# Weight scales of a recursive matmul layer taken out of the step list that forms its weights, and later fetches cut into pieces

## The chip, the cores and the metric

The kernel runs on one core of a Trainium2 chip. The metric is device time in microseconds for one launch, as the median of several runs. A profile is one execution of the same program, read by the hardware profiler. Five engines work side by side, each from its own queue in order: TensorE (PE: matmuls, with its weight loads in PEld), VectorE (DVE), ScalarE (ACT), GpSimd (POOL) and SyncE (SP), which here only issues transfers. A queue stands still while its first instruction waits.

## The reference, cut to what matters

```python
def _moe_ref(x, w1, w2, w3, w_out):        # x: the attention's output, 1792 x 768
    h = (x @ w1) * (x @ w2) @ w3
    return h @ w_out
def _moe2_ref(x, w_in, w_out):             # w_in 768 x 2048, w_out 2048 x 768
    r = np.maximum(x @ w_in, 0.0)
    return (r * r) @ w_out
```

Talking-heads attention comes first, then these two layers. The change lies in the second one: its input layer is `x @ w_in` with the squared ReLU, its output layer is the product with `w_out`.

## The kernel before, in words

All matmuls of the two layers work on numbers split into a high and a low float16 half; a product of two such numbers takes three matmuls (high by high, high by low, low by high). To split a tensor, it is first scaled by a power of two taken from its largest magnitude; ACT then writes the high half and DVE the low half. The program calls the pair a cast.

**Stages.** Attention fills the first 450 us or so, the hidden layer and a merged weight matrix follow. The product that makes the second layer's tokens (L1179, source `M16` and `hs`) runs next, in four blocks `i` of 448 tokens. The input layer follows (L1782, `multiply_in`), then the output layer (L2004, `multiply`).

**The input layer** uses Winograd's recursive scheme on two by two blocks: seven products in place of eight. It runs 16 items `SEQ[n] = (q, t)`: eight quads `q` (each a pair of 128-column chunks of `w_in`) by two halves `t` of the tokens. An item is seven products of nine matmuls. The last two products of an item (`in3`, `in4`) are issued within the next item. A product's sum is read from PSUM by `take_in` into a tile `ev` (L1817 on ACT, L1819 on DVE) with a scale `scs[n]` (tile `sci`, L1952 on DVE, at the item's start). Product S2 adds onto the tile of A11, and S1 onto that of S2, so TensorE may go on there only when ACT has read the tile.

**What an item needs.** Its quad must be formed: the two chunks are read back from DRAM (`sides`, `ib<-kept_in`, L1016), POOL makes four sums (L1019), and four casts write the quad's halves (L1065 on ACT, L1066 on DVE). Their scale comes from the largest magnitude of a group of four chunks (`top`, L1005): `crossing` sends that number through DRAM, with two transfers that POOL issues (L820, L824), and a DVE chain (`pow2`, L108 to L113) makes the power of two. The tokens need the same: `x2_steps` finds their scale (a PE transpose L1580, a DVE maximum, a PE spread L1588, a DVE chain), then POOL makes sums (L1595) and 21 casts per half write `x` (L1370, L1366). The first half of the tokens lies in `xb`; the mixed output weights are later loaded over it.

**What sets the order.** The program is issued as Python runs, and the order in each queue is written by step lists. A step list (`Stream`) yields pairs of an engine and an estimated cost. `tick(us)` after a product moves an estimated clock `now` and lets every list, in the order of `streams` and the weight decoding last, issue steps whose engine's estimated backlog is at most `ahead[0]` (3 us here). `REST` is a pause in that clock; `after(eng)` is a pause until the engine's estimated backlog is gone. `finish(st)` issues a list's remaining steps at once without pauses; `need(key)` does so with the weight decoding, `need_in(q)` with `form_in`. Transfers of results are kept in `puts` and issued on SP's queue when their estimated time has come, or by `flush`. `allow[0]` is how far the decoding of weight chunks may go; `IN_M` sets it for this part.

**Lists that matter here.** `form_in` forms the quads in order, with each group's `top`, `crossing` and scale ahead of its two quads. Before the first item the program calls `need_in(0)` and `need_in(1)`. At quad 0 `form_in` calls `finish(x_of[0])`, the first half's tokens. `mixed_out(0)` makes the mixed output weights for the output layer's first half (L1696, L1700, L1701) and stores them in `ow_d`; `load_mixed` reads them back in one go during item 14 (L1768). `mixed_tokens` reads the squared results back (`gt<-g`, L1880), makes sums on POOL (L1897) and casts `ao` (L1916 on ACT, L1917 on DVE).

Of the kernel before, what the change touches and what calls it, by code (L numbers as in the profile page):

```python
# [10 lines left out]
F32 = mybir.dt.float32  # L11
# [3 lines left out]
ALU = mybir.AluOpType  # L15
# [3 lines left out]
P = 128  # L19
# [15 lines left out]
def talking_heads_attention_moe_moe2(  # L35
# [678 lines left out]
    NA = NFC - 2  # L714
    IN_M = 14
    chunks += [("in", j) for j in range(12)] + [("out", j) for j in range(NA, OG)]
# [232 lines left out]
    def one_steps(i):  # L949
# [15 lines left out]
        if kind in ("in", "out"):  # L965
            sums = in_sums[:, j : j + 1] if kind == "in" else out_sums[j // OG][:, j % OG : j % OG + 1]
            x, ops = decode(t, n, sums)
            yield from read_raw(i, x, ops)
            yield POOL, 0, lambda: put_later(DVE, "kept", (kept_in if kind == "in" else kept_out)[j], x)
            wsp[kind, j] = True  # L970
            return
        x, ops = decode(t, n)
# [22 lines left out]
    def flat(t):  # L995
        return t.rearrange("p a d -> p (a d)").bitcast(F32)

    def form_in():

        for g in range(NF2 // IG):  # L1000
            box = {}
            a = sm.tile([P, 1], F32, tag="im", name="im")

            def top():
                nc.vector.tensor_reduce(  # L1005
                    a, in_sums[:, g * IG : (g + 1) * IG], axis=AX.X, op=ALU.max
                )

            def scale():
                box["scale"] = pow2(largest_sent(box.pop("sent"), 1), 13, "is")  # L1010

# [8 lines left out]

            while ("in", (g + 1) * IG - 1) not in wsp:
                yield REST, 0.5, lambda: need(("in", (g + 1) * IG - 1))
            yield after(ACT)
            yield DVE, 0.3, top
            yield from crossing(a, 1, box, DVE)
            yield DVE, 0.8, scale
            up, lo = box["scale"]
            for q in range(g * IG // 2, (g + 1) * IG // 2):
                if q == 0:
                    while not x_of:  # L1030
                        yield REST, 0.5, lambda: None
                    finish(x_of[0])
                yield POOL, 0, lambda: sides(q)
# [4 lines left out]
                for o, l, r, op in (  # L1038
                    (ta[:, :OH], a21, a22, ALU.add), (ta[:, OH:], ta[:, :OH], a11, ALU.subtract),
                    (tb[:, :OH], a11, a21, ALU.subtract), (tb[:, OH:], a12, ta[:, OH:], ALU.subtract),  # L1040
                ):
                    yield POOL, 1.1, lambda: mix(o, l, r, op)
                if q:
                    while not fin_pool or (q > 2 and over[0] < q - 1):
# [16 lines left out]
                for x, (h, l) in parts:  # L1061
                    n = x.shape[-1] // OH
                    if x is ta:
                        yield after(POOL)
                    yield ACT, 0.5 * n, lambda: nc.scalar.activation(h, x, AF.Copy, scale=up)  # L1065
                    yield DVE, 0.9 * n, lambda: nc.vector.scalar_tensor_tensor(  # L1066
                        l, x, up, h, op0=ALU.mult, op1=ALU.subtract
# [498 lines left out]
    xbig = []  # L1566

    def xop(t, z, k, c):
        if t == 0:
            return xs_[z][:, k, c]  # L1570
        if k == T4:
# [3 lines left out]
    def x2_steps(t, ts, xm):  # L1575
# [45 lines left out]
        )  # L1621
        yield after(DVE)
        yield POOL, 0, turned
        yield REST, 0.3, None
        yield DVE, 0.25, top
        yield REST, 0.3, None
        yield POOL, 0, spread
# [48 lines left out]
    def mixed_out(g):  # L1676
# [21 lines left out]
        def cast(x, h, l, n):  # L1698
            up = box["up"]
            yield ACT, 0.5 * n, lambda: nc.scalar.activation(h, x, AF.Copy, scale=up)  # L1700
            yield DVE, 0.9 * n, lambda: nc.vector.scalar_tensor_tensor(  # L1701
                l, x, up, h, op0=ALU.mult, op1=ALU.subtract
# [49 lines left out]

    def load_mixed():
        finish(mixed[0])
        flush("ow")
        load_part((B11, B21, T2, T3, T1, B22))
        for q in range(NQ):
            ow[0, q] = [ow_s[q // 2][:, k, q % 2] for k in range(7)]

    ow_s = [  # L1760
# [3 lines left out]

    def load_part(ks):
        for k in ks:
            for z in range(2):
                nc.sync.dma_start(ow_s[z][:, k], ow_d[k][:, 2 * z : 2 * z + 2])  # L1768

# [124 lines left out]
    def mixed_tokens():  # L1894
# [4 lines left out]
        for n in range(2 * NTT):  # L1899
# [9 lines left out]
            a21, a22, a11, a12 = (qs[key] for key in ((1, 0), (1, 1), (0, 0), (0, 1)))  # L1909
            yield REST, lambda: max(0.0, qs["at"] + 6.0 - now[0]), None  # L1910

# [32 lines left out]

    need_in(1)
    streams.append(mixed_out(0))
    for n, (q, t) in enumerate(SEQ):
# [10 lines left out]
        if n:  # L1958
            in3(n - 1)
        y = mm(0)  # L1960
        multiply_in(y, n, A12, B21, True)
# [5 lines left out]
        if n and SEQ[n - 1] == (NP2 - 1, 0):  # L1967
            load_mixed()
        if n and SEQ[n - 1] == (NP2 // 2 - 1, 1):
# [3 lines left out]
        st_[n] = event()  # L1973
        take_in(x, n, None, st_[n])
        tick(0.57, 0.65)
        z = zt_[n] = mm(0)
        multiply_in(z, n, S3, T3, True)
        tick(0.57)
        multiply_in(x, n, S1, T1, False)
        s4 = event()  # L1980
        take_in(x, n, None, s4)
        take_in(z, n, s4, s4)
        g_tile(n, 1, 1, s4, DVE)
        tick(0.57, 0.65, 0.68)
        if n == len(SEQ) - 4:
            streams.append(tokens)
    in3(len(SEQ) - 1)
    in4(len(SEQ) - 1)
    load_part((T4,))
    g_scales[1] = Stream(g_scale(1, gms[1]))  # L1990
# [181 lines left out]
```

## Time and profile before

| what | us |
|---|---|
| median of 3 runs | 1275.64 (1274.67 to 1278.06) |
| the profiled execution, own time | 1276.11 |
| the profiled execution, span | 1274.4 |
| TensorE busy in the span | 1219.5 |

The span goes from the first instruction to the last; the profiled execution's own time is 1.7 us longer. Busy TensorE time includes matmuls at a lowered clock, so both idle time and slow time have to be read. The page's clock row gives the granted clock as a share of full speed; a row of matmuls shows the idle time ahead of it in brackets, with the instruction that ended it.

### The profile page before, as it was taken

What the parts mean: (1) busy time and instruction counts of PE and PEld (TensorE: products, weight loads), DVE (VectorE), ACT (ScalarE), POOL (GpSimd) and SP (SyncE); (2) the same over time, 40 slices, a digit from 0 to 9 for tenths busy, and PEclk for the clock granted to TensorE, in tenths of its full rate; (3) what the DMA queues carried; (4) which work ended last, traced back from release to release, by engine and by line L of the source; (5) the groups of instructions that cost most, each with busy time, mean ns of one, the idle gap of its engine ahead of it and who ended that gap; (6) DMA issues with size and microseconds to landing.
All of it is one profiled execution on the core that took longest, in us unless ns stands there. A gap on an engine that the chain in (4) does not pass through costs nothing.

```text
span 1274.4 us, 26177 instructions
## 1 busy us (share of the span) xinstructions
PE 1219.5 (96%) x9884; PEld 747.7 (59%) x9884; DVE 945.5 (74%) x1721; ACT 804.6 (63%) x1626; POOL 594.1 (47%) x585
## 2 busy tenths in 40 slices
PE   8999999999999999999999999987989996999998
PEld 4666776766666655555579754533445553556565
DVE  6988898798799757765756355857777843899773
ACT  6888888888887536554546465756656653666330
POOL 4898798798787300010014005234124402887350
PEclk9999999999999999999999999988999997999999
DMA  6466456555556726655335171633796875757562
GB/s 195 125 166 168 117 156 166 137 143 143 162 162 167 229 57 153 165 126 157 132 103 168 65 186 65 231 111 100 238 254 152 308 265 145 206 167 226 162 188 87
DMA packets 140354, 205.54 MB, mean 161 GB/s; under 512 B 34148, under 2 KB 115172, under 8 KB 140228
## 3 DMA queue, kind: packets, MB, share of 16 engines
q1 hardware_dynamic: 136020, 200.01, 53.7%
q0 software_dynamic: 1072, 1.45, 0.8%
q10 hardware_dynamic: 3136, 2.40, 0.7%
q8 instruction: 78, 1.28, 0.4%
q14 instruction: 48, 0.39, 0.1%
HBM read 115.12 MB, written 50.17 MB: 130 GB/s over the span
## 4 chain that ended last, share of the span: by engine, by line
PE 75%; DMA 8%; DVE 8%; ACT 5%; issue 2%; SPq 1%; POOL 1%; ACTq 0%; DVEq 0%; POOLq 0%
PE mm L1179 20%; PE mm L2004 13%; PE p L284 10%; PE mm L1782 8%; PE o L380 8%; PE mm L1454 5%; PE s L241 5%; PE a L494 4%; DVE x L1366 2%; DMA g<-ev 2%; DMA Bt<-S 2%; PE p L1179 2%; DMA gt<-g 1%; DMA ib<-kept_in 1%; DVE ATl L402 1%
## 5 line engine op out<-in xcount | busy, mean ns | idle before, releaser
L1782 PE MATMUL mm<-x,wq 128*128 128x448 f16 x882 | 179.3, 365 | 25.5 <-ACT ev L1817 13.4
L1179 PE MATMUL mm<-x,w 128*128 128x448 f16 x1044 | 197.7, 352 | 0.0
L1179 PEld LDWEIGHTS <-w 128*128 128x128 f16 x1152 | 112.2, 98 | 104.3
L2004 PEld LDWEIGHTS <-ao 128*128 128x128 f16 x1176 | 115.3, 98 | 83.9 <-issue 4.4
L284 PE MATMUL p<-Bt,wpre_k 120*120 120x448 f32 x360 | 159.0, 559 | 4.3 <-DMA Bt<-S 3.9
L1782 PEld LDWEIGHTS <-wq 128*128 128x128 f16 x882 | 88.4, 101 | 114.9 <-issue 25.7
L380 PEld LDWEIGHTS <-EH 120*112 120x112 f16 (+1 forms) x1440 | 124.4, 130 | 44.7 <-issue 37.3
L353 POOL TENSOR_SCALAR EH<-E,st 120x448 f16<-120x448 f32 (+1 forms) x152 | 113.0, 752 | 46.8 <-DVE st L336 34.8
L402 DVE TENSOR_TENSOR ATl<-o,ATh 112x480 f16<-112x480 f32 x180 | 116.1, 645 | 23.2 <-ACT ATh L396 22.4
L306 ACT ACTIVATE E<-p,st 120x448 f32<-120x448 f32 x180 | 116.0, 644 | 21.8 <-DVE st L298 13.2
L396 ACT CAST ATh<-o 112x480 f16<-112x480 f32 x180 | 101.1, 561 | 44.4 <-PE o L380 39.7
L380 PE MATMUL o<-wph,EH 120*112 120x120 f16 x720 | 124.0, 219 | 1.3 <-DVE ATl L402 1.3
L380 PE MATMUL o<-wph,EL 120*112 120x120 f16 x720 | 122.0, 216 | 0.0
L380 PE MATMUL o<-wpl,EH 120*112 120x120 f16 x720 | 122.0, 216 | 0.0
L365 POOL TENSOR_TENSOR EL<-F,EH 120x448 f16<-120x448 f32 (+1 forms) x90 | 104.2, 1158 | 33.2 <-issue 20.2
L298 DVE TENSOR_REDUCE st<-p 120x1 f32<-120x448 f32 x180 | 110.2, 613 | 2.2 <-PE p L284 1.9
L1179 PE MATMUL mm<-h,M 128*128 128x448 f16 x576 | 109.8, 353 | 0.7 <-ACT M L1370 0.6
L2004 PE MATMUL mm<-x,ao 128*128 128x384 f16 x588 | 98.2, 329 | 4.2 <-ACT ao L1916 2.9
L2004 PE MATMUL mm<-ow,ao 128*128 128x384 f16 x588 | 96.4, 326 | 1.4 <-DVE st L2020 1.4
L380 PEld LDWEIGHTS <-EL 120*112 120x112 f16 x720 | 93.6, 130 | 0.0
L782 DVE SCALAR_TENSOR_TENSOR xa<-zt,xa 128x768 int32<-128x768 int32 (+1 forms) x70 | 70.1, 1001 | 31.1 <-ACT zt L774 27.5
L367 DVE SCALAR_TENSOR_TENSOR EL<-E,st,EH 120x448 f16<-120x448 f32 (+1 forms) x90 | 83.2, 925 | 10.9 <-POOL EH L353 10.5
(262 smaller groups left out, 2518.8 us busy)
## 6 DMA issues: line engine op xcount, KB each, us to landing
Bt<-S SPq DMA_DIRECT2D x176, 210.0 KB
raw<-in_moe_w_out_dram SPq DMA_DIRECT2D x24, 768.0 KB
g<-ev SPq DMA_DIRECT2D x64, 224.0 KB
gt<-g SPq DMA_DIRECT2D x56, 256.0 KB
raw<-in_moe_w_in_dram SPq DMA_DIRECT2D x16, 768.0 KB
raw<-in_moe_w_dram SPq DMA_DIRECT2D x14, 768.0 KB
raw<-in_moe_w_dram SPq DMA_DIRECT2D x16, 512.0 KB
kept_out<-xa SPq DMA_DIRECT2D x16, 384.0 KB
```

The source lines that it names most:

```text
L284: nc.tensor.matmul(pt[: n * H, :S], wpre_k.rearrange("p t g -> p (t g)")[: n * H, : n * H], Bt.pop(u)[: n * H], start=True, stop=True,)
L298: nc.vector.tensor_reduce(nsum[u][:n, 0, j : j + 1], Pp[u][:n, :S], axis=AX.X, op=ALU.max, negate=True)
L306: nc.scalar.activation(e[:n], Pp.pop(u)[:n, :S].rearrange("p (a b) -> p a b", a=EG), AF.Exp, bias=t[:n, 0, j : j + 1], scale=1.0, accum_ou ...
L353: nc.gpsimd.tensor_scalar(seven(EH[u][:n]), Ex[u][:n], inverse(u), 1.0, op0=ALU.mult, op1=ALU.mult)
L365: nc.gpsimd.tensor_tensor(a, f, b, op=ALU.subtract)
L367: nc.vector.scalar_tensor_tensor(a, e, inverse(u), b, op0=ALU.mult, op1=ALU.subtract)
L380: nc.tensor.matmul(pt[:CP, c * n : (c + 1) * n], a[:n, c * CP : (c + 1) * CP], w[:n, :n], start=(i == 0), stop=(i == 2),)
L396: nc.scalar.copy(ATs[s][0][:, :, :, m * NR : m * NR + nr], src)
L402: nc.vector.tensor_tensor(ATs[s][1][:, :, :, a], src, ATs[s][0][:, :, :, a], op=ALU.subtract)
L1179: nc.tensor.matmul(pt[:, :S], w[a][:, cs], x[z][:, sl], start=(c == 0 and i == 0), stop=(c == len(parts) - 1 and i == 2),)
L1782: nc.tensor.matmul(pt[:, :S], w[:, a, c * P : (c + 1) * P], xop(t, b, kb, c), start=(start and c == 0 and m == 0), stop=(c == 2 and m == 2 ...
L2004: nc.tensor.matmul(pt[:, :OH], y[:, a, q * P : (q + 1) * P], ow[g, q][kb][:, w], start=(start and q == 0 and m == 0), stop=(q == NQ - 1 an ...
```

## The change

The scale of each group gets a step list of its own (`in_scale`), started when the group's last chunk is decoded. `form_in` reads a quad's chunks and makes its sums as soon as those two chunks are decoded, and asks for the scale only ahead of the casts. `need_in(1)` ahead of the items goes, and `finish(x_of[0])` within `form_in` becomes a pause until that list has ended (it is still called when the list is forced). `IN_M` is 16 instead of 14. The token scale's list gets pauses ahead of its two PE steps. Three DVE cast costs are estimated at 0.55 instead of 0.9. The mixed output weights are read back in seven pieces, in the order in which the output layer uses them (`USE`; the first half of the tokens is laid out in the same order), one after each product that read the tokens below them for the last time. The second token tile of the output layer is fetched in item 15, the `mixed_tokens` list starts one item earlier, and its first tile pauses 10 us after its fetch instead of 6.

```diff
-    IN_M = 14
+    IN_M = 16
...
             wsp[kind, j] = True
+            if kind == "in" and j % IG == IG - 1:
+                scaling.append(Stream(in_scale(j // IG)))
+                streams.append(scaling[-1])
...
+    scaling, in_scales = [], {}
+
+    def in_scale(g):
+        box = {}
+        a = sm.tile([P, 1], F32, tag="im", name="im")
...
+        def scale():
+            in_scales[g] = pow2(largest_sent(box.pop("sent"), 1), 13, "is")
+
+        yield after(ACT)
+        yield DVE, 0.3, top
+        yield from crossing(a, 1, box, DVE)
+        yield DVE, 0.8, scale
+
+    def have_scale(g):
+        need(("in", (g + 1) * IG - 1))
+        finish(scaling[g])
...
-            while ("in", (g + 1) * IG - 1) not in wsp:
-                yield REST, 0.5, lambda: need(("in", (g + 1) * IG - 1))
-            yield after(ACT)
-            yield DVE, 0.3, top
-            yield from crossing(a, 1, box, DVE)
-            yield DVE, 0.8, scale
-            up, lo = box["scale"]
             for q in range(g * IG // 2, (g + 1) * IG // 2):
-                if q == 0:
-                    while not x_of:
-                        yield REST, 0.5, lambda: None
-                    finish(x_of[0])
+                while ("in", 2 * q + 1) not in wsp:
+                    yield REST, 0.5, lambda: need(("in", 2 * q + 1))
                 yield POOL, 0, lambda: sides(q)
...
+                while g not in in_scales:
+                    yield REST, 0.5, lambda: have_scale(g)
+                up, lo = in_scales[g]
+                if q == 0:
+                    while not x_of:
+                        yield REST, 0.5, lambda: None
+                    while x_of[0] in streams:
+                        yield REST, 0.5, lambda: finish(x_of[0])
...
-                    yield DVE, 0.9 * n, lambda: nc.vector.scalar_tensor_tensor(
+                    yield DVE, 0.55 * n, lambda: nc.vector.scalar_tensor_tensor(
...
+    USE = (B11, B21, T2, T3, T1, B22, T4)
+
     def xop(t, z, k, c):
         if t == 0:
-            return xs_[z][:, k, c]
+            return xs_[z][:, USE.index(k), c]
...
         yield after(DVE)
+        yield REST, 2.0, None
         yield POOL, 0, turned
         yield REST, 0.3, None
         yield DVE, 0.25, top
-        yield REST, 0.3, None
+        yield after(DVE)
+        yield REST, 0.8, None
         yield POOL, 0, spread
...
-    def load_mixed():
-        finish(mixed[0])
-        flush("ow")
-        load_part((B11, B21, T2, T3, T1, B22))
+    def load_mixed(i):
+        if i == 0:
+            finish(mixed[0])
+            flush("ow")
...
+        for z in range(2):
+            puts.append((now[0] + 1.5, "mixed", ow_s[z][:, i], ow_d[USE[i]][:, 2 * z : 2 * z + 2]))
...
-            yield REST, lambda: max(0.0, qs["at"] + 6.0 - now[0]), None
+            yield REST, lambda: max(0.0, qs["at"] + (6.0 if n else 10.0) - now[0]), None
...
-    need_in(1)
     streams.append(mixed_out(0))
...
             in4(n - 1)
         if n and SEQ[n - 1] == (NP2 - 1, 0):
-            load_mixed()
+            load_mixed(5)
+        if n == len(SEQ) - 1:
+            load_tokens(1)
+        going = SEQ[n] == (NP2 - 1, 0)
+        if going:
+            load_mixed(0)
...
-        if n == len(SEQ) - 4:
+        if n == len(SEQ) - 5:
             streams.append(tokens)
...
-    load_part((T4,))
+    load_mixed(6)
+    flush("mixed")
```

Pieces 1, 2 and 3 follow the later products of item 13 in the same way, and piece 4 follows `in3` in item 14.

## Rows read from the trace of the kernel before

**Rows 1.** The page: its first line and TensorE's busy time.
```profile
span 1274.4 us, 26177 instructions
...
PE 1219.5 (96%) x9884; PEld 747.7 (59%) x9884; DVE 945.5 (74%) x1721; ACT 804.6 (63%) x1626; POOL 594.1 (47%) x585
```

**Rows 2.** Busy time by stretch: length, busy us (xcount) per engine, clock, DMA share, GB/s.
```profile
1071.00:1271.00 200.00, 194.37 (x1181) 115.47 (x1179) 152.22 (x192) 88.23 (x138) 108.16 (x72) 0.99 0.61 176
833.00:892.00 59.00, 44.30 (x202) 20.78 (x200) 39.62 (x70) 33.88 (x63) 26.11 (x24) 0.86 0.31 93
892.00:948.00 56.00, 54.89 (x290) 28.07 (x287) 44.35 (x78) 37.48 (x75) 10.83 (x10) 1.00 0.85 254
948.00:1018.00 70.00, 63.87 (x324) 32.15 (x325) 55.88 (x92) 44.26 (x82) 33.61 (x28) 0.95 0.72 222
1018.00:1117.00 99.00, 83.05 (x439) 44.29 (x439) 57.54 (x89) 48.54 (x89) 34.49 (x25) 0.91 0.71 206
```

**Rows 3.** Timeline, TensorE, 700 to 1120 us: start, length; idle before, its releaser.
```profile
777.37 0.27 PE L1580 MATMUL mm<-ident,xm 128*1 128x128 f32 x1 [1.62 <-DVE xm L1619]
...
841.55 7.28 PE L1782 MATMUL mm<-x,w 128*128 128x448 f16 x27 [5.10 <-ACT ev L1817]
...
868.41 0.93 PE L1782 MATMUL mm<-x,wq 128*128 128x448 f16 x2 [5.56 <-ACT wq L1065]
...
952.90 0.93 PE L1782 MATMUL mm<-x,wq 128*128 128x448 f16 x2 [4.91 <-ACT wq L1065]
...
1057.58 3.39 PE L1782 MATMUL mm<-x,wq 128*128 128x448 f16 x9 [6.83 <-ACT ev L1817]
1065.68 6.14 PE L1782 MATMUL mm<-x,wq 128*128 128x448 f16 x18 [4.71 <-ACT ev L1817]
...
1084.51 0.78 PE L2004 MATMUL mm<-x,ao 128*128 128x384 f16 x2 [2.94 <-ACT ao L1916]
```

**Rows 4.** Windows of 8 us, TensorE alone: length, busy (xcount), granted clock, DMA.
```profile
952.00:960.00 8.00, 6.19 (x21) 0.61 0.14 31
```

**Rows 5.** Timeline, ScalarE, 740 to 880 us.
```profile
834.61 1.42 ACT L1065 ACTIVATE wq<-ib,is 128x768 f16<-128x768 f32 x2
835.94 1.75 ACT L1065 ACTIVATE wq<-it,is 128x768 f16<-128x768 f32 x2
840.86 0.63 ACT L1817 ACTIVATE ev<-mm,sci 128x448 f32<-128x448 f32 x1 [3.18 <-DVE sci L1952]
```

**Rows 6.** Timeline, VectorE, 740 to 880 us.
```profile
784.43 1.56 DVE L1366 SCALAR_TENSOR_TENSOR x<-tm,xs,x 128x448 f16<-128x448 f32 x1
...
840.62 0.15 DVE L1952 TENSOR_TENSOR sci<-kx,is 128x1 f32<-128x1 f32 x1
...
861.53 1.88 DVE L1366 SCALAR_TENSOR_TENSOR x<-st,xs,x 128x448 f16<-128x448 f32 x3 [0.28 <-ACT x L1370]
...
866.66 0.15 DVE L108 TENSOR_SCALAR is<-acr 128x1 f32<-128x1 f32 x1
```

**Rows 7.** Timeline, GpSimd, 720 to 900 us.
```profile
843.32 0.56 POOL L820 DMA_DIRECT2D across<-im  x1 [4.89 <-DVE om L1683]
```

**Rows 8.** Timeline, VectorE, 880 to 960 us.
```profile
927.75 0.15 DVE L1005 TENSOR_REDUCE im<-isum 128x1 f32<-128x4 f32 x1
```

**Rows 9.** Timeline, SyncE's DMA queue, 840 to 1120 us: start, issuing time.
```profile
945.79 1.21 SPq L1016 DMA_DIRECT2D ib<-kept_in  x2
...
1034.69 7.75 SPq L1768 DMA_DIRECT2D x<-ow_d  x12
...
1044.91 4.74 SPq L1880 DMA_DIRECT2D gt<-g  x4
```

**Rows 10.** Timeline, ScalarE, 960 to 1110 us.
```profile
1054.48 1.50 ACT L1916 ACTIVATE ao<-gt,gs 128x512 f16<-128x512 f32 x2 [9.17 <-DMA gt<-g]
```

**Rows 11.** Windows around the fetches at the layer's end, columns as in group 2.
```profile
1018.00:1040.00 22.00, 21.76 (x116) 11.25 (x116) 15.47 (x27) 13.86 (x29) 0.00 (x0) 1.00 0.60 212
1040.00:1056.00 16.00, 10.75 (x57) 5.47 (x56) 2.15 (x5) 4.19 (x9) 2.27 (x2) 0.93 1.06 371
```

More of the change, by code (lines that the diff above doesn't have):

```diff
@@ L996, in flat, with top @@
         return t.rearrange("p a d -> p (a d)").bitcast(F32)
+    scaling, in_scales = [], {}
+    def in_scale(g):
+        box = {}
+        a = sm.tile([P, 1], F32, tag="im", name="im")
+        def top():
+            nc.vector.tensor_reduce(
+                a, in_sums[:, g * IG : (g + 1) * IG], axis=AX.X, op=ALU.max
+            )
+        def scale():
[7 more added lines that the diff above has]
+        finish(scaling[g])
     def form_in():
@@ L1001, in form_in @@
             box = {}
[L1002 to L1010, printed above, removed]
             def sides(q):
@@ L1700, in cast @@
             yield ACT, 0.5 * n, lambda: nc.scalar.activation(h, x, AF.Copy, scale=up)
-            yield DVE, 0.9 * n, lambda: nc.vector.scalar_tensor_tensor(
+            yield DVE, 0.55 * n, lambda: nc.vector.scalar_tensor_tensor(
                 l, x, up, h, op0=ALU.mult, op1=ALU.subtract
@@ L1751, in mixed_out @@
         return mixed[g]
-    def load_mixed():
-        finish(mixed[0])
-        flush("ow")
-        load_part((B11, B21, T2, T3, T1, B22))
-        for q in range(NQ):
-            ow[0, q] = [ow_s[q // 2][:, k, q % 2] for k in range(7)]
     ow_s = [
@@ L1763, in talking_heads_attention_moe_moe2 @@
     ]
[L1765 to L1768, printed above, removed]
+    def load_mixed(i):
+        if i == 0:
+            finish(mixed[0])
+            flush("ow")
+            for q in range(NQ):
+                ow[0, q] = [ow_s[q // 2][:, USE.index(k), q % 2] for k in range(7)]
+        for z in range(2):
+            puts.append((now[0] + 1.5, "mixed", ow_s[z][:, i], ow_d[USE[i]][:, 2 * z : 2 * z + 2]))
     gms = [sm.tile([P, OG, B], F32, tag="gm", name="gm") for _ in range(2)]
@@ L1959, in talking_heads_attention_moe_moe2 @@
             in3(n - 1)
+            if SEQ[n - 1] == (NP2 - 1, 0):
+                load_mixed(4)
         y = mm(0)
@@ L1974, in talking_heads_attention_moe_moe2 @@
         take_in(x, n, None, st_[n])
+        if going:
+            load_mixed(1)
         tick(0.57, 0.65)
@@ L1977, in talking_heads_attention_moe_moe2 @@
         multiply_in(z, n, S3, T3, True)
+        if going:
+            load_mixed(2)
         tick(0.57)
         multiply_in(x, n, S1, T1, False)
+        if going:
+            load_mixed(3)
         s4 = event()
```

## The prediction

> **What bounds the kernel now.** First the page: TensorE is busy 96% of the span [rows 1], so only its idle and its slow time can be won. Then the windows by stage, where the reader is to see that the loss is local. In the undisturbed stretch, 892 to 948, 290 matmuls of 448 columns take 54.89 us of busy time at full clock, 0.189 us each; the output layer's 384 columns take 194.37 / 1181 = 0.165 us [rows 2]. Against these rates:
>
> - 833 to 892 (the input layer's first items): idle 59.0 - 44.3 = 14.7 us; 202 matmuls should take 38.2 us and take 44.3, so 6.1 us are slow clock (0.86).
> - 892 to 948: idle 1.1 us, clock 1.00.
> - 948 to 1018: idle 6.1 us; 324 matmuls should take 61.3 and take 63.9, 2.5 us slow.
> - 1018 to 1117 (the seam of the two layers): idle 15.9 us; some 200 matmuls of 448 columns and 239 of 384 should take 77.2 us and take 83.05, 5.9 us slow.
>
> That is 52.4 us, and 1.6 us stand ahead of it at 777. Next the timeline of TensorE, for what ended each gap [rows 3]: an eviction by ACT (5.10 at 841, 6.83 and 4.71 at 1057 and 1065), a quad's cast (5.56 at 868, 4.91 at 952), a token cast (2.94 at 1084). Last the 8 us windows: the one that follows the gap at 952 ran at 0.61, close to the lower level of 1.2 GHz [rows 4], while the 1.1 us lost before 948 left the clock at 1.00 [rows 2]. So a long gap costs twice and a short one once.
>
> **The change part by part.**
>
> *Token scale pauses.* The transpose at 777 waited 1.62 us on DVE [rows 3]. With 2.0 us of pause it is issued later, among matmuls that have work. Bounds: 0 to 1.6 gained. What hides it is the running product; if the DVE chain is later than the pause, a part comes back. I take 1.2.
>
> *need_in(1) gone (gap at 841).* ACT ran quad 1's four high halves at 834.6 to 837.7, then waited 3.18 us for `sci`, which stood on DVE behind the four low halves [rows 5, 6]; only then came the eviction that TensorE waited for. After the change `sci` is issued ahead of those casts. But the casts aren't gone: `form_in` may issue them at the first two ticks, and their estimated ACT cost of 3.5 us fits nearly whole into the 3 us of backlog allowed. So ACT still runs about 3.1 us of casts first, and the eviction ends near 834.6 + 3.1 + 0.6 = 838.4 instead of 841.5. The gap shrinks from 5.1 to about 2.0. Bounds: 0 left if the casts land behind the eviction, 5.1 if nothing changes.
>
> *Scales apart (gaps at 868 and 952).* Group 1's number left for DRAM at 843.3 [rows 7] and its scale chain started at 866.7 [rows 6]: 23 us, all of it after quad 1's casts, and quad 2 waited for it. Group 2's `top` ran at 927.8 [rows 8], quad 4's chunks were asked for only at 945.8 [rows 9], and TensorE stood at 948. Now the number of group 1 can travel from the moment its fourth chunk is decoded; `IN_M` 16 lets that happen in block 1 instead of block 2. The crossing leaves the path, and reads and sums of a quad follow the last quad's casts directly: for quad 4 some 18 us earlier (945.8 - 927.8). What is late next is the quad itself: fetch, POOL sums, casts, and for quads 3 on the wait for a free tile.
>
> *The first items get crowded.* This is what I charge against the gain. DVE is busy 39.6 us in 833 to 892 [rows 2], and TensorE needs only 38.2 us there at full rate. One chunk's decoding (about 2.5 us of DVE) moves ahead of 833 with `IN_M`, so 37 us of DVE must fit into 38. The second half of the tokens has to be ready at item 3, and its list stands ahead of the quads in the order. I leave 5 us of waits beside the 2.0, and 3 us of slow clock. Bounds: 0 and the 12.7 idle now left over (14.7 - 2.0); I take 5 since the work just fits. The stretch then gives 20.8 - 10 = 10.8 us.
>
> Here the Trainium skill speaks against the change. A token cast on DVE takes 1.56 us while POOL makes sums (784.4) and 1.88 / 3 = 0.63 us when it doesn't (861.5) [rows 6]. The Trainium skill, SBUF — State Buffer, section "Who interferes with whom", says that GpSimd and VectorE share one port pair and that it is an exclusive lock; the rows agree in direction. By that rule the 26 us of POOL in this stretch can't lie under DVE's two-operand work, and a shorter stretch packs them closer: at worst the stretch stays near 50 us and gives 9 instead of 10.8, a sum 1.8 us higher.
>
> *948 to 1018.* With quad 4's reads 18 us earlier the 4.91 should go but for a remainder; quads 5 to 7 gain likewise. I leave 1.8 us idle and 0.7 slow of 8.6: gain 6.1. Bounds: 0 (the fetch is as late as before, behind other entries of SP's queue) and 8.6. The stretch 892 to 948 I leave as it is.
>
> *DVE estimates of 0.55.* They remove no instruction and add none; the lists may issue more DVE work per tick, and an eviction or `sci` can stand behind more of it. Cost: nothing where TensorE has 27 matmuls (5.1 us) between a product and the next use of its tile, all of it in a rival below.
>
> *Fetches in pieces, earlier.* SP issued the twelve reads of the output weights in one block from 1034.7 to 1042.4 and the first tokens' four reads right behind it, from 1044.9 [rows 9]. Their `ao` cast stood at the head of ACT's queue for 9.17 us, until 1054.5 [rows 10], with evictions behind it: hence 6.83 and 4.71. In that time the DMA engines were full (share 1.06 in 1040 to 1056) while 1018 to 1040 had 40% free [rows 11]. The pieces start an item earlier, the last weight chunks are decoded two items earlier, and the first tokens' fetch no longer follows a block of twelve. Each piece waits on SP's queue for the product that reads its tile; behind it wait result stores and the tokens' fetch, a few us at most. The twelve reads carry 4.7 MB, at 371 GB/s 12.7 us of the engines; the free share before 1040 is 8.8 us, so some 4 us still fall where they did. I leave 4 us idle at the seam, 1.5 at 1084 and after (the second tile is fetched an item earlier), 2.5 slow, 8 of 21.8: gain 13.8. Bounds: 0 and 21.8.
>
> Sum: 1.2 + 10.8 + 0 + 6.1 + 13.8 = 31.9. The profiled execution took 1276.1 us, 0.5 above the median of the runs: 1276.1 - 31.9 = 1244.2, so 1244 for the median.
>
> **The rivals.**
>
> 1. *The gaps move.* The crossing goes, but quads 2 and 4 are then late by fetch and sums, the first items are DVE-bound, and `ao` still waits for a full DMA. For it: DVE 39.6 against 38.2, DMA share 1.06. Against it: from 892 to 948 the same kinds of casts, fetches and evictions ran with 1.1 us idle. The stretches give 5, 2 and 5 us with the 1.2: 1276 - 13 = 1263. Chance 0.20.
>
> 2. *All cover holds.* Every gap over 2 us goes and the clock stays up: the losses left are about 2 at 836, 1.1, and 5 elsewhere, so 54 - 8 = 46 won: 1230. For it: the clock's share (14.5 us) goes by itself with the long gaps. Chance 0.10.
>
> 3. *Slower: evictions behind a deeper DVE queue.* Place: the starts of items 4 to 12, where `sci` and the last eviction of the item before must pass DVE within 5.1 us. With estimates of 0.55, a backlog of 3 estimated us holds five casts of 384 columns; beside POOL at the 1.56 us of rows 6 that is 7.8 us, 2.7 too many. If every one of 16 items pays it, that is 43 us, all 32 gained and 11 more: 1287. It decides against the change from 2.0 us per item. Against it: DVE was busy 44.3 of 56 us from 892 to 948 [rows 2], so its queue runs empty between, and POOL only 10.8. Chance 0.09.
>
> 4. *The change does nothing measurable:* the lists wait for the same decoding and the forced `need_in` calls restore the old order. 1275. Against it: `sci` and the crossing change place for certain. Chance 0.05.
>
> The forecast itself, 1236 to 1254, has 0.56.
>
> **How the numbers follow.** A difference under 0.3% (3.8 us) can't be told from none. Forecast and rivals 1 and 2 are faster: 0.86; rival 4 is the same, 0.05; rival 3 slower, 0.09. The low end, 1229, takes in rival 2's figure; the high end, 1267, takes rival 1 with all bounds of the seam but the worst. Outside are rivals 3 and 4 and a little of 2, under 0.2.
>
> **What would show it.** In the profile after: no `wq` cast that waits for a scale chain, and `top` of group 1 well ahead of the first item; TensorE's first gap in the input layer near 2 us, ended by ACT; the 833 to 892 work done in about 48 us; output weight reads spread over some 20 us, and an `ao` wait on ACT under 5 us; the clock near 1.0 from the first item to the output layer. Wrong would be: a new wait on `x` casts at item 3 over 8 us; a piece's wait on SP that holds the token fetch; `sci` starting late in the items where nothing waited before.

## The result, and the profile after

The changed kernel took 1258.42 us (median of 4 runs, 1256.89 to 1261.17), the kernel before 1276.2 in the runs beside it (4 runs): 17.8 us less, a ratio of 0.9862 with a 95% interval of 0.984 to 0.9885. The forecast was 1244, the range 1229 to 1267. The sign and the range held; the forecast's own range of 1236 to 1254 didn't, and 14 of the 32 us stayed away. The time lies nearer to rival 1's 1263 than to the forecast, though not for the reason that rival 1 gave.

The profiled execution after took 1261.17, the slowest of its four; its span is 1259.5 us, 14.9 us shorter than the one before, and TensorE is busy 1214.7 us of it.

The stretches of [rows 2] in the kernel after (length; busy us and count of PE, PEld, DVE, ACT, POOL; granted clock, DMA share, GB/s):

```profile
833.00:892.00 59.00, 47.53 (x218) 22.86 (x216) 49.84 (x80) 37.21 (x71) 28.35 (x23) 0.88 0.46 135
892.00:948.00 56.00, 49.74 (x255) 25.07 (x254) 46.93 (x75) 36.89 (x71) 20.48 (x16) 0.97 0.80 261
948.00:1018.00 70.00, 63.61 (x334) 32.54 (x333) 50.83 (x84) 46.63 (x90) 26.91 (x23) 1.00 0.68 218
1018.00:1117.00 99.00, 97.00 (x562) 54.87 (x561) 65.46 (x96) 54.78 (x96) 44.03 (x32) 1.00 0.65 203
```

The stretches hold other work now, so count matmuls: 218 instead of 202 in the first, 255 instead of 290 in the second, 334 instead of 324 in the third. The stretch that I had left as it is lost 35. Only in the fourth did both idle and slow clock go: 97.00 of 99 us busy at 1.00, against 83.05 at 0.91. The timeline of TensorE shows it gap by gap (start, length; idle before, its releaser), the counterpart of [rows 3]:

```profile
841.15 1.28 PE L1800 MATMUL mm<-x,w 128*128 128x448 f16 x3 [5.50 <-ACT ev L1835]
...
870.23 6.95 PE L1800 MATMUL mm<-x,wq 128*128 128x448 f16 x27 [3.17 <-DVE ev L1837]
879.79 2.50 PE L1800 MATMUL mm<-x,wq 128*128 128x448 f16 x9 [2.61 <-ACT ev L1835]
...
920.22 3.56 PE L1800 MATMUL mm<-x,wq 128*128 128x448 f16 x18 [2.76 <-ACT ev L1835]
...
935.95 25.43 PE L1800 MATMUL mm<-x,wq 128*128 128x448 f16 x126 [3.22 <-ACT ev L1835]
964.57 3.56 PE L1800 MATMUL mm<-x,wq 128*128 128x448 f16 x18 [3.19 <-ACT ev L1835]
```

What the reader is to see: no gap is ended by a `wq` cast any more (5.56 and 4.91 before), and from 1018 to 1117 none is over 1.3 us (6.83, 4.71 and 2.94 before). But the gap at 841 stands, and from 870 to 965, where two gaps near 5 us stood before, five of about 3 us wait for an eviction. (Item 4 starts at 895, item 8 at 951, item 13 at 1018.)

To compare kernels whose stages shift, I divide each one's timeline of TensorE by the count of matmuls: item 0 has 45 of 448 columns, every other item 63, and 18 close the layer; the output layer is divided after 588 of its 1176. Each boundary is the start of the first matmul of the next stage. (Interpolating inside a merged row of the timeline isn't good enough: in the kernel before, the row that holds item 13's start also holds the slow clock after the gap at 952, and the boundary comes out 2.4 us late. The expectations below were worked out with boundaries of that kind, so where they have 53.4 us for items 13 to 15 before, the table has 55.8.) The token product is the stage ahead of the input layer. Times are us.

| kernel | token product | items 0-3 | 4-12 | 13-15, tail | output, 1st half | 2nd half | median us | ratio to before (95%) |
|---|---|---|---|---|---|---|---|---|
| before | 112.6 | 66.0 | 116.9 | 55.8 | 101.8 | 97.4 | 1276.2 | |
| after | 110.3 | 63.1 | 122.5 | 40.0 | 100.8 | 97.5 | 1258.42 | 0.9862 (0.984-0.9885) |
| seam_only | 112.6 | 65.7 | 116.4 | 40.1 | 98.3 | 98.8 | 1259.45 | 0.9867 (0.984-0.9894) |
| scales_only | 110.8 | 60.3 | 123.1 | 40.0 | 109.4 | 97.9 | 1266.73 | 0.9927 (0.9905-0.9949) |
| est09 | 112.0 | 64.3 | 110.5 | 40.8 | 95.6 | 100.9 | 1249.02 | 0.9779 (0.9749-0.9809) |
| inm14 | 110.3 | 59.1 | 121.8 | 40.0 | 100.8 | 97.5 | 1254.57 | 0.9831 (0.9803-0.9859) |
| est09_mixed | 111.3 | 61.5 | 116.0 | 40.0 | 95.6 | 99.2 | 1249.74 | 0.9815 (0.9795-0.9835) |
| abs_later | 110.3 | 62.9 | 125.6 | 40.0 | 100.8 | 97.5 | 1264.49 | 0.9926 (0.9914-0.9939) |
| no_pause | 112.0 | 59.6 | 124.0 | 40.0 | 100.8 | 97.8 | 1259.69 | 0.9881 (0.9864-0.9897) |
| est09_inm14 | 110.3 | 60.0 | 117.5 | 41.8 | 99.9 | 99.2 | 1250.56 | 0.9826 (0.9805-0.9848) |
| ahead_lo | 114.4 | 66.0 | 116.5 | 40.0 | 102.0 | 98.9 | 1262.9 | 0.9915 (0.9897-0.9933) |
| est09_gact | 114.5 | 58.6 | 114.9 | 44.9 | 95.5 | 98.9 | 1253.34 | 0.9837 (0.9817-0.9856) |
| est09m_inm14 | 110.3 | 59.1 | 113.9 | 41.2 | 95.6 | 100.7 | 1246.81 | 0.9787 (0.9767-0.9807) |
| est09m_gact | 111.8 | 59.2 | 115.7 | 40.0 | 95.6 | 100.8 | 1248.66 | 0.9801 (0.978-0.9821) |

One of est09's six runs, 1271.35 us at a granted clock of 0.945, was slow and is left out of its median and ratio.

At 0.189 us a matmul the three stages of the input layer would take 44.3, 107.3 and 39.1 us without a loss. So the layer's end is now clean (40.0), items 0 to 3 are 19 us over and items 4 to 12 are 15 over. Between the two profiled executions the stages give 2.3 + 2.9 - 5.5 + 15.8 + 1.0 - 0.1 = 16.4; the unchanged stretch ahead of the token product was 1.5 longer after, which leaves the 14.9 of the span.

How well does one execution's stage repeat? The kernels after, scales_only and est09_mixed give every engine and SyncE's queue the same instructions in the same order from the token product to the end of item 3. There they took 110.3, 110.8 and 111.3 us in the product and 63.1, 60.3 and 61.5 us in items 0 to 3, and the first gap of the input layer, 5.50 us in the kernel after, was shorter in the two others (scales_only first):

```profile
836.68 0.73 PE L1801 MATMUL mm<-x,w 128*128 128x448 f16 x3 [2.75 <-ACT ev L1836]
837.58 0.73 PE L1800 MATMUL mm<-x,w 128*128 128x448 f16 x3 [3.42 <-ACT ev L1835]
```

est09 and est09_gact share their order through the product, and it took 112.0 and 114.5 us. So a difference of less than some 3 us between two stages of single executions shows nothing by itself.

### The profile page after: what moved, and what is told of

It reads as the page before. It is cut to its first block, busy times and chain, and to the rows that moved or that the text cites. A ratio compares the mean times of both kernels' runs of the same rounds, so it can differ in the third digit from the quotient of the medians.

```text
span 1259.5 us, 26176 instructions
## 1 busy us (share of the span) xinstructions
PE 1214.7 (96%) x9884; PEld 747.0 (59%) x9884; DVE 944.1 (75%) x1721; ACT 803.7 (64%) x1626; POOL 592.3 (47%) x585
## 3 DMA queue, kind: packets, MB, share of 16 engines
q8 instruction: 78, 1.28, 0.4%
## 4 chain that ended last, share of the span: by engine, by line
PE 73%; DVE 13%; ACT 5%; DMA 5%; issue 3%; POOL 1%; SPq 0%; ACTq 0%; DVEq 0%
PE mm L1196 20%; PE mm L2035 10%; PE p L284 9%; PE mm L1800 9%; PE o L380 8%; PE mm L1471 5%; PE s L241 5%; PE a L494 4%; DVE x L1383 2%; DMA Bt<-S 2%; PE p L1196 2%; DVE xa L778 1%; DVE ow L1722 1%; DMA ow_d<-st 1%; ACT wq L1082 1%
## 5 line engine op out<-in xcount | busy, mean ns | idle before, releaser
L1800 PE MATMUL mm<-x,wq 128*128 128x448 f16 x882 | 173.7, 358 | 19.3 <-ACT ev L1835 16.2
L396 ACT CAST ATh<-o 112x480 f16<-112x480 f32 x180 | 101.1, 562 | 46.0 <-PE o L380 40.8
L782 DVE SCALAR_TENSOR_TENSOR xa<-zt,xa 128x768 int32<-128x768 int32 (+1 forms) x70 | 72.7, 1038 | 26.0 <-ACT zt L774 22.3
```

Of the source, the lines that this page charges most:

```text
L396: nc.scalar.copy(ATs[s][0][:, :, :, m * NR : m * NR + nr], src)
L1800: nc.tensor.matmul(pt[:, :S], w[:, a, c * P : (c + 1) * P], xop(t, b, kb, c), start=(start and c == 0 and m == 0), stop=(c == 2 and m == 2 ...
```

## The experiments

My theory after the result: the seam is worth what was forecast, the scales apart are worth little by themselves, and the estimates of 0.55 and `IN_M` 16 cost time that they were charged nothing for. The rival: one of the two large parts works against the other, and neither number matters.

**seam_only.** The kernel before with the fetches in pieces alone:

```
+    USE = (B11, B21, T2, T3, T1, B22, T4)
+        if n == len(SEQ) - 1: load_tokens(1)
+        going = SEQ[n] == (NP2 - 1, 0)
+        if going: load_mixed(0)      # pieces 1 to 6 likewise
-        if n == len(SEQ) - 4:
+        if n == len(SEQ) - 5:
             streams.append(tokens)
```

> The kernel before with the later fetches alone: mixed output weights read back in seven pieces, token tile 1 fetched in item 15, the token list one item earlier with its 10 us. If the seam's gain stands by itself (theory): the last three items drop from 53.4 to about 40 us, and the output layer isn't slowed by denser casts, so about 1276 - 13 - 4 = 1259. If it needs the earlier decoding that IN_M 16 brings (rival): the first token tile is still late, 1268 to 1272.

Measured: 1259.45, with items 13 to 15 at 40.1 instead of 55.8. The seam alone gives as much as the whole change (ratios 0.9867 and 0.9862). Which of its three edits does it (pieces, the token list an item earlier, the second tile in item 15) was not taken apart.

**scales_only.** The kernel after without these fetches: pauses, `in_scale`, `IN_M` 16, 0.55, no `need_in(1)`.

> The changed kernel without the later fetches: scale lists apart, no need_in(1), IN_M 16, pauses, estimates of 0.55. Theory (the scale part gives back by new waits in items 4 to 12 and in the output layer what it wins at 777 and in items 0 to 3): 2.3 + 2.9 won, 3.1 and about 3 lost, so 1274 to 1278, no change. Rival (the two parts help each other, the seam hides nothing of this part): 1266 to 1270.

Measured: 1266.73, so my theory fell. The time is the rival's, but its reason, that the parts help each other, isn't seen. The scale part isn't worth nothing: it empties items 13 to 15 too (40.0), and it pays 7.6 us in the first half of the output layer (109.4 against 101.8) and 6.2 in items 4 to 12. By ratio the two parts alone win 0.0133 + 0.0073, some 26 us; together 17.8. They overlap by about 9 us, and the place is the seam: over items 13 to 15 and the output layer's first half seam_only wins 19.2 us, scales_only 8.2 and both together 16.8.

**est09.** The kernel after with the old estimates:

```
-                    yield DVE, 0.55 * n, lambda: nc.vector.scalar_tensor_tensor(
+                    yield DVE, 0.9 * n, lambda: nc.vector.scalar_tensor_tensor(
```

in `form_in` and in `mixed_out`'s cast. The change lowers the estimate in these two lines, not in three. Nothing else differs: the same instructions, issued at other points.

> The changed kernel with the three VectorE estimates back at 0.9. Theory (the lists issue casts too densely at 0.55; ScalarE's sum in the weight decoding and evictions then wait behind them): the new waits of 2.8, 3.2 and 3.2 us in items 5 to 10 shrink to under 1 each and the output layer's 1.3 us waits per token tile go, so 1246 to 1251. Rival (the waits come from the work packed together, GpSimd sums beside VectorE casts, whatever the estimate): 1256 to 1260, the waits stay.

Measured: 1249.02; its interval lies below that of the change. Items 4 to 12 take 110.5 instead of 122.5 us, and the first half of the output layer 95.6 instead of 100.8. Waits of TensorE from 700 to 1260 us by releaser (us in total, times, longest), the kernel after first:

```profile
PE mm L1800 <- ACT ev L1835: 21.7, 11, 5.5
PE mm L2035 <- DVE st L2051: 5.3, 5, 1.3
```

and est09:

```profile
PE mm L1800 <- ACT ev L1835: 8.9, 7, 3.2
PE mm L1800 <- DVE x L1383: 5.8, 1, 5.8
PE mm L1800 <- ACT x L1387: 3.3, 1, 3.3
PE mm L2035 <- DVE st L2051: 3.2, 2, 2.5
```

Waits for evictions fall from 21.7 to 8.9 us (of those expected to shrink to under 1, 1.20 and 1.67 us are left at 920 and 984). What appears instead is a wait for the second tokens' casts at item 3 (5.8 and 3.3).

**inm14.** The kernel after with `IN_M = 14`.

> The changed kernel with IN_M back at 14. Theory (the two chunks decoded ahead of the input layer hold ScalarE back, so the eviction of item 0 starts 2.7 us later than the casts alone make it): the first gap falls from 5.5 to about 2.5 us, but the same decoding then lies in items 1 to 4; 1255 to 1258. Rival (the earlier decoding is what makes the seam's fetches early): the first tokens come later and the seam loses 3 to 8 us, 1261 to 1266.

Measured: 1254.57, and items 0 to 3 at 59.1 instead of 63.1; the gap at 841 becomes 1.52 (at 835.8). The totals' intervals overlap, so only the stage tells it. It is 59.1 in est09m_inm14 too, which has the same order there, and the first gap is 1.52 in all three runs with 14. Against the three executions of one order named above (60.3 to 63.1) the gain is 1.2 to 4.0 us.

**est09_mixed.** Only `mixed_out`'s cast gets its 0.9 back.

> The changed kernel with the estimate of 0.9 in mixed_out alone; form_in keeps 0.55. Theory (it is the mixed output weights' casts that fill VectorE's queue in items 4 to 12 and in the output layer, since 28 of them are issued per layer half): nearly all of the gain of the run with all estimates at 0.9, items 4 to 12 near 111 us instead of 122 and the first half of the output layer near 96 instead of 101; 1248 to 1251. Rival (the quads' casts ahead of the items are the ones that block): 1254 to 1258.

Measured: 1249.74. The first half of the output layer comes down to 95.6 by this alone, items 4 to 12 only to 116.0. By ratio 6 of est09's 10.6 us come from this one number; the other 4.6 aren't certain, since the two intervals overlap. Over all runs the number decides items 4 to 12: the six with 0.9 here take 110.5 to 117.5 us, the five with 0.55 and the old limit on the backlog 121.8 to 125.6.

**abs_later.** A theory of how 0.55 costs: in items 4 to 12 ScalarE takes a step of a chunk's decoding (`zt`) that waits for VectorE, with an eviction behind it on ScalarE. The step is put 2.5 us later:

```
         x, ops = decode(t, n, sums)
+            ops.insert(-1, (REST, 2.5, None))
```

> The changed kernel with one more pause of 2.5 us in the decoding of the second layer's weight chunks, ahead of ScalarE's sum of magnitudes; estimates stay at 0.55. Theory (that sum stands at the head of ScalarE's queue while VectorE is late, and the evictions wait behind it): ScalarE's waits for the decoded chunk fall from 7.8 to under 2 us in 890 to 1020, and items 4 to 12 from 122 to 114 to 117 us; the output layer keeps its 1.3 us waits; 1250 to 1254. Rival (VectorE is late in any case and the evictions wait for its scale product or for the tiles it frees): items 4 to 12 stay at 120 or more, 1256 to 1260.

Measured: 1264.49, slower; the theory fell. ScalarE's waits from 890 to 1020 us in the kernel after:

```profile
ACT zt L789 <- DVE xa L782: 7.8, 4, 2.8
ACT ev L1835 <- DVE sci L1969: 7.3, 4, 4.4
```

and in abs_later, where lines are one higher:

```profile
ACT ev L1836 <- DVE sci L1970: 12.4, 6, 4.6
```

The wait of `zt` is gone, and ScalarE now waits more for `sci` and, in its ReLU, for VectorE's own eviction (7.0 us against 4.3). So ScalarE's order was a symptom: it waits for a VectorE that is late, whichever operation stands at the head.

**no_pause.** The token scale pauses taken out again (`REST, 2.0`, `after(DVE)`, and 0.3 for 0.8).

> The changed kernel without the two pauses in the token scale's list. Theory (the pauses alone took the 1.6 and 0.5 us ahead of the two steps on TensorE at 777, and 1.1 at 851): the token product goes from 110.3 back to 112.5 us and items 0 to 3 lose about 1; 1260 to 1262. Rival (the list is no longer forced, so the steps come apart without the pauses): 1257 to 1259.

Measured: 1259.69, not to be told from the change. The product is back at 112.0; the small products of the two token scale chains wait 1.65 us at 782 and 4.2 at 840, and items 0 to 3 still take only 59.6.

**est09_inm14.** Both numbers back.

> The changed kernel with all VectorE estimates at 0.9 and IN_M at 14. Theory (the two are independent: 9.2 from the one, 3.9 from the other): 1244 to 1247. Rival (with 0.9 the first items are no longer held by the two chunks ahead of them, so 14 only makes the later decoding late): 1248 to 1252.

Measured: 1250.56, as the rival had it. The two gains don't add: items 0 to 3 come to 60.0, and items 4 to 12 are 117.5 instead of 110.5. The loss lies in items 4 to 7 (56.9 against 49.0). That the chunks decoded later cause it isn't shown: est09_gact, with `IN_M` 16, has 55.0 there.

**ahead_lo.** The rival on 0.55: not which list is dense, but how much work may stand in VectorE's queue. The limit scaled down with the estimates (3.0 times 0.55 / 0.9 is 1.83; I took 1.65):

```
-    ahead[0] = 3.0
+    ahead[0] = 1.65
```

> The changed kernel with estimates of 0.55 but a backlog of 1.65 us allowed instead of 3.0 from the token product on, so that as many casts may stand in VectorE's queue as with 0.9 and 3.0. Theory (the depth of VectorE's queue ahead of an eviction is what costs): items 4 to 12 fall from 122 to about 112 us and the output layer's 1.3 us waits per token tile shrink; 1247 to 1253. Rival (what costs is that the list of the mixed output weights runs off too early and too fast, whatever the depth): items 4 to 12 stay above 119, 1255 to 1262.

Measured: 1262.9, slower than the change. Items 4 to 12 improve to 116.5, between what the two sides expected, but the product (114.4), items 0 to 3 (66.0) and the output layer pay for it. The limit holds for every list, 0.55 only for two, so this run doesn't tell whether depth ahead of an eviction is what costs in items 4 to 12.

**est09_gact, est09m_gact.** Items 0 to 3 keep VectorE busy, so eight of their ReLU tiles go to ScalarE, on top of est09 and est09_mixed:

```
-        g_tile(n, 0, 0, s1, DVE)
+        g_tile(n, 0, 0, s1, ACT if n < 4 else DVE)
-        g_tile(n, 1, 1, s4, DVE)
+        g_tile(n, 1, 1, s4, ACT if n < 4 else DVE)
```

> The run with all estimates at 0.9, and in items 0 to 3 the two squared-ReLU tiles that VectorE made per item are made by ScalarE: 8 tiles of about 0.7 us leave VectorE. Theory (items 0 to 3 are bound by VectorE, busy 48 of 59 us there): they fall from 64 to 58 to 60 us, 1243 to 1246. Rival (ScalarE's own evictions, which TensorE waits for first, are what binds): they stay or grow, 1249 to 1255.

> Estimate 0.9 in mixed_out alone, and the squared-ReLU tiles of items 0 to 3 on ScalarE. Theory (VectorE binds the first items): items 0 to 3 fall from 61.5 to 57 to 59 us, 1245 to 1248. Rival (ScalarE's evictions bind): 1250 to 1255.

Measured: 1253.34 and 1248.66. Items 0 to 3 come down as expected (58.6 and 59.2), but with est09 the total is no better: items 4 to 12 (114.9) and the layer's end (44.9) take more than in est09. The 114.5 of the product isn't the edit's, for the product's order is est09's. With est09_mixed the total can't be told from est09_mixed itself.

**est09m_inm14.** 0.9 for `mixed_out` alone, and `IN_M` 14.

> Estimate 0.9 in mixed_out alone, 0.55 in form_in, IN_M at 14. Theory (with the quads' casts issued early, the two chunks fewer shorten items 0 to 3 as they did with 0.55 everywhere): 1245 to 1248. Rival (as with 0.9 everywhere, the decoding that is put off lands in items 4 to 7): 1249 to 1253.

Measured: 1246.81, the lowest median: 2.1% under before, and its interval lies wholly below that of the change. Against est09 it is not shown to be faster (0.9787 and 0.9779). Its largest gaps left in the input layer are two waits for token casts at item 3 (3.22 us at 873.7 and 2.60 at 876.8) and one for an eviction at 914.6 (3.10).

## Why the prediction was right in sign and short in size

**The sum.** By stage: token product 1.2 us forecast, 2.3 measured; items 0 to 3, 10.8 and 2.9; items 4 to 12, 6.1 forecast and 5.5 lost; the seam, 13.8 and 16.8. Two terms fell 8 and 12 us short. That the total stayed in its range owes 3 us to a seam that gave more than its term.

**The seam: right, and a little more.** 13.8 us forecast up to 1117; 15.8 measured in items 13 to 15 and 1.0 in the first half of the output layer. SyncE's queue after (start, issuing time) shows the twelve reads of [rows 9] in four steps over 15 us, and the first tokens' fetch ahead of them instead of behind:

```profile
1000.10 2.17 SPq L1898 DMA_DIRECT2D gt<-g  x4
1021.80 0.80 SPq L1161 DMA_DIRECT2D x<-ow_d  x2
1025.20 5.18 SPq L1161 DMA_DIRECT2D x<-ow_d  x6
1033.15 0.98 SPq L1161 DMA_DIRECT2D x<-ow_d  x2
1036.55 0.80 SPq L1161 DMA_DIRECT2D x<-ow_d  x2
```

The first `ao` casts ran from 1015.8 with no wait, where 9.17 us stood in [rows 10]. I left 8 us of loss there; 2 are left (99.0 - 97.0). That the part is worth this by itself, seam_only shows (15.7 and 3.5).

**The token pauses: right in sign.** 1.2 forecast; 1.3 to 2.3 in the three executions of the same order, of which no_pause gives back 0.7 to 1.7. That is near what one execution differs by, so the size isn't shown. In est09, with the pauses, the product took 112.0.

**need_in(1): the move happened, its gain didn't.** I had ScalarE run 3.1 us of casts from 834.6 and the eviction right behind, a gap of 2.0. `sci` did come early, and the scale chain with it (VectorE):

```profile
829.70 0.15 DVE L108 TENSOR_SCALAR is<-acr 128x1 f32<-128x1 f32 x1
...
834.10 0.15 DVE L1969 TENSOR_TENSOR sci<-kx,is 128x1 f32<-128x1 f32 x1
```

The casts took their 3.1 us, but started at 837.50, for ScalarE was late (its timeline):

```profile
826.52 0.91 ACT L774 ACTIVATE zt<-raw 128x768 f32<-128x768 f32 x1 [2.80 <-DMA raw<-in_moe_w_in_dram]
...
831.32 0.84 ACT L789 ACTIVATE zt<-xa 128x768 f32<-128x768 f32 x1 [2.67 <-DVE xa L782]
...
837.50 1.43 ACT L1082 ACTIVATE wq<-ib,is 128x768 f16<-128x768 f32 x2
838.83 1.75 ACT L1082 ACTIVATE wq<-it,is 128x768 f16<-128x768 f32 x2
840.49 0.61 ACT L1835 ACTIVATE ev<-mm,sci 128x448 f32<-128x448 f32 x1
```

The two chunks that `IN_M` 16 lets in just ahead of the layer cost 5.47 us of waits at ScalarE's head, one of them for a chunk's transfer. In scales_only, with the same order, these two waits are 1.33 and 2.15 us and the gap is 2.75: part of the 5.50 is this execution's bad luck. I had counted one chunk's decoding moved out of the first items as relief; inm14 shows that it moved onto their first eviction: without it the gap is 1.52.

**Scales apart, 833 to 892: the crossing left the path, the size failed.** Group 1's maximum is taken at 808.8 and its scale stands at 829.7, both ahead of item 0, and the 5.56 us wait on `wq` is gone. I left 10 us of loss (2.0 for the first gap, 5 for crowding, 3 for slow clock) and kept a gain of 10.8; items 0 to 3 won 2.9, in scales_only 5.7. The first gap (5.50 instead of 2.0, but 2.75 in scales_only) is 0.8 to 3.5 of what is missing. VectorE is a likely bound for a part: it was busy 49.84 us of the 59, against 39.62 before, for only 16 more matmuls. But with ReLU tiles moved off it (est09_gact) it was busy 36.0 of 58.6 us and the stage was still 14 us over the ideal, so its load alone doesn't explain what remains; that wasn't settled.

**"DVE estimates of 0.55 ... cost nothing": the step that failed.** It is the place that rival 3 named, evictions behind a deeper VectorE queue in items 4 to 12, at a smaller price: est09 shows 12.0 us there and 5.2 in the first half of the output layer, 3.4 of them given back in the second, where rival 3 had 43. I set it at nothing because a product has 5.1 us of cover at each tile, and because VectorE was busy only 44 of 56 us. The average hid where the work lands. The 28 casts of `mixed_out`'s first half ran on VectorE from 914.1 to 1000.1 before, from 910.1 to 971.6 after, and from 910.6 to 999.7 in est09, and the last store left SyncE's queue at 1007.17, 972.32 and 998.79: with 0.55 the list starts no sooner but ends some 30 us sooner, and is denser. The gap at 935.95 in the kernel after, VectorE first:

```profile
926.23 0.94 DVE L1969 TENSOR_TENSOR sci<-kx,is 128x1 f32<-128x1 f32 x1
927.09 1.43 DVE L1722 SCALAR_TENSOR_TENSOR st<-ob,os,st 128x384 f16<-128x384 f32 x1
928.45 1.35 DVE L775 TENSOR_SCALAR xa<-raw 128x768 int32<-128x768 int32 x1
929.72 1.35 DVE L1722 SCALAR_TENSOR_TENSOR st<-ob,os,st 128x384 f16<-128x384 f32 x1
...
932.78 1.63 DVE L782 SCALAR_TENSOR_TENSOR xa<-zt,xa 128x768 int32<-128x768 int32 x1
934.34 0.60 DVE L1722 SCALAR_TENSOR_TENSOR st<-ot,os,st 128x384 f16<-128x384 f32 x1
```

GpSimd at that time:

```profile
925.77 1.37 POOL L1717 TENSOR_TENSOR ot<-ob 128x384 f32<-128x384 f32 x1
927.11 0.99 POOL L1717 TENSOR_TENSOR ot<-ob,ot 128x384 f32<-128x384 f32 x1
928.07 1.31 POOL L1037 TENSOR_TENSOR it<-ib 128x384 f32<-128x384 f32 x1
929.46 1.19 POOL L1037 TENSOR_TENSOR it<-it,ib 128x384 f32<-128x384 f32 x1
...
931.90 1.70 POOL L1037 TENSOR_TENSOR it<-ib,it 128x384 f32<-128x384 f32 x1
```

and ScalarE:

```profile
934.45 0.84 ACT L789 ACTIVATE zt<-xa 128x768 f32<-128x768 f32 x1 [2.49 <-DVE xa L782]
...
935.29 0.61 ACT L1835 ACTIVATE ev<-mm,sci 128x448 f32<-128x448 f32 x1
```

A cast that the list reckons at 0.55 takes 1.35 to 1.43 while GpSimd sums and 0.60 at 934.34, after the last sum ended (931.90 + 1.70). The decoding step on VectorE is late behind them, ScalarE waits 2.49 us for it, and the eviction that TensorE needs comes 3.22 us late. The Trainium skill, SBUF — State Buffer, section "Who interferes with whom", which the prediction weighed at 1.8 us in the first items, states that these two engines share a port pair under an exclusive lock; the rows of this gap agree.

But the longer casts aren't what 0.55 adds. VectorE's casts of this list from 895 to 1018, the kernel after first, then est09 (count; busy us, mean ns of one):

```profile
L1722 DVE SCALAR_TENSOR_TENSOR st<-ob,os,st 128x384 f16<-128x384 f32 x12 | 11.3, 960 | 2.2 <-ACT st L1721 2.2
L1722 DVE SCALAR_TENSOR_TENSOR st<-ot,os,st 128x384 f16<-128x384 f32 x16 | 9.2, 611 | 0.1
L1722 DVE SCALAR_TENSOR_TENSOR st<-ob,os,st 128x384 f16<-128x384 f32 x12 | 11.0, 933 | 2.4 <-ACT st L1721 2.4
L1722 DVE SCALAR_TENSOR_TENSOR st<-ot,os,st 128x384 f16<-128x384 f32 x16 | 9.1, 613 | 4.6 <-ACT st L1721 4.6
```

The same 28 casts cost VectorE the same with either estimate; 0.9 only spaces them. That the spacing is worth the time, est09 and est09_mixed show. Why a denser list delays evictions is read from this one gap, and is not shown for the others.

In the output layer the same list's second half is dense too. VectorE before the gap of 1.28 us at 1115.72:

```profile
1108.48 2.76 DVE L1722 SCALAR_TENSOR_TENSOR ow<-ob,os,ow 128x384 f16<-128x384 f32 x2
1111.17 3.97 DVE L1722 SCALAR_TENSOR_TENSOR ow<-ot,os,ow 128x768 f16<-128x768 f32 x2
1115.06 0.60 DVE L2051 SCALAR_TENSOR_TENSOR st<-mm,sv,st 128x384 f32<-128x384 f32 x1
```

Four casts in a row, 6.7 us, stand ahead of an eviction; three such gaps of 1.28 us follow each other at 15.5 us.

**948 to 1018: the wait went, the gain only in est09.** 6.1 us forecast here and nothing in 892 to 948; items 4 to 12 lost 5.5. The wait of 4.91 on `wq` is gone, as forecast. With the old estimates they won 6.4 in est09, the forecast's size, but the five other runs with 0.9 in `mixed_out` lie between 0.6 lost and 3.0 won. So the term was covered by the one above, and how much of it is there without 0.55 isn't settled.

**Rivals.** Rival 1 came nearest in time; its first half (items bound by VectorE) is seen at most in part, its second (`ao` still waits for a full DMA) isn't seen at the seam. Rival 2's clean profile didn't come. Rival 4 is out by the interval.

**Open.** Why est09 and inm14 don't add is shown only as to place (items 4 to 7), not as to cause, and no run here tells what keeps items 0 to 3 at 58.6 us and more.

## What to carry to other kernels

In a hand-written order the cost estimate of a filler operation is a spacing: lowering it to the operation's duration alone made the same work end sooner and in clumps here, so change it in a run of its own, and look at which stage the clump lands in. Charge a step that is moved ahead of a stage to the queue that runs into that stage, not only as relief to the one it leaves. Two edits that each clear the same stall aren't worth their sum; run each alone before adding terms. Before a stage's few microseconds are explained, look for two kernels with the same order there and see how far they differ.

## What the runs showed of the hardware that was not expected

The lengthening beside GpSimd's sums doesn't go by size. The 128x1 product `sci`, with two tensors as operands, took 0.94 us at 926.23, inside the sum that began at 925.77, and 0.15 at 834.10. Of the 16 in the kernel after, five took 0.94 to 1.07 us, each begun inside a sum, and the others 0.16 at most (two of 16 in the kernel before). VectorE's timeline at 851.75:

```profile
851.75 1.07 DVE L1969 TENSOR_TENSOR sci<-kx,is 128x1 f32<-128x1 f32 x1
...
852.93 0.15 DVE L109 TENSOR_SCALAR xs<-xs 128x1 int32<-128x1 int32 x1
```

and GpSimd:

```profile
851.29 1.52 POOL L1614 TENSOR_TENSOR st<-st 128x448 f32<-128x448 f32 x1
852.77 1.12 POOL L1614 TENSOR_TENSOR tm<-st,tm 128x448 f32<-128x448 f32 x1
```

`sci` ends as the first sum does (852.81), and an operation on one tensor of the same size takes 0.15 us inside the next. A scale of one column can be as late as a whole cast. Nor is an operation on one tensor always spared: the decoding step of 128x768 took 0.55 us at 831.20, with GpSimd idle, and 1.35 at 928.45 in the gap above, where GpSimd's sums ran.

A gap of some 3 us was followed by either level of the granted clock. TensorE's 4 us windows in which the gaps ended, at 870.23 (3.17 us) and 964.57 (3.19 us) in the kernel after (length, busy (xcount), granted clock, DMA share, GB/s):

```profile
870.00:874.00 4.00, 3.77 (x12) 0.58 0.00 0
964.00:968.00 4.00, 3.43 (x18) 1.00 1.01 379
```

After the gap of 3.22 us at 935.95 the clock was 0.64 from 936 to 940, and after 2.76 us at 920.22 it stayed at 1.00. So the length of one gap alone didn't tell which level follows.
